# One-operation variances in the tail, half of the h rows ahead of the LN3 sums, and keys of two more pairs on ScalarE

## The chip, the cores and the metric

The kernel runs on one core of a Trainium2 chip. The metric is device time of one execution in microseconds (us); lower is better. The recorded span of an execution is the stretch that the profile covers; the time is about 1.8 us longer. A measurement of the kernel before gave 286.26 us, median of 3 runs, 286.24 to 286.33.

Some words: a look is one profiled execution. The granted clock is the share of its full rate that TensorE was given, by the profile's own record; half clock is 0.50 there and full clock 1.00. A load lands when its completion is signalled, a little after its last packet (0.41 us for the last weights in before, 0.36 us in the look of the tail alone). PSUM is the memory that this kernel's matmuls write into, SBUF the one that its loads land in.

## The reference, cut to what matters

One decode step of one token: attention over a 4096-key window of a cache with 32 heads, then a gated MLP, each behind a layer norm without gain.

```python
x = A_x                                                        # 1 x 1 x 640
h = x + A(layernorm(x), k_cache, v_cache, wq, wo)              # 32 heads of 192, last 4096 keys
h2 = h + B(layernorm(h), w_in, w_sp, b_sp, w_out)
# B: z = gelu(x @ w_in); z1, z2 = halves; z2 = layernorm(z2)
#    g = w_sp * z2 + b_sp  (one token: w_sp and b_sp are scalars);  out = (z1 * g) @ w_out
```

LN1, LN2 and LN3 below are the norms of x, of h and of z2. Most bytes are keys and values: 16 pairs of heads with 3 MB of keys and 3 MB of values each; 119.35 MB are loaded in all.

## The kernel before: what the change and the argument touch

The keys of a pair are multiplied by the query on VectorE, then summed over the 192 channels: by matmuls with the identity on TensorE, with some columns taken over by ScalarE (`BY_ACT`) or VectorE (`BY_DVE`).

```python
BY_ACT = (0, 1, 3, 5, 7, 9, 11)     # 16 of 32 key columns of the first half of these pairs on ScalarE
BY_DVE = (2, 4, 6, 8, 10, 12)

def add_on_act(t, part):            # 8 columns each call, one activation per column
    ...
    for j in range(j0, j0 + JS // 2):
        nc.scalar.activation(out=k3[:, j, :], in_=k3[:, j, :], func=ACT.Copy, accum_out=S[:, j:j + 1])
```

The reciprocal root is an integer seed and two Newton steps, each of two one-column VectorE operations:

```python
def ln_rstd(hv):                    # hv = -variance / 2
    yi = ...                        # seed: tensor_scalar on the bits, two immediate scalars
    for _ in range(2):
        scalar_tensor_tensor(out=t_, in0=y, scalar=y, in1=hv, op0=mult, op1=mult)
        scalar_tensor_tensor(out=yn, in0=t_, scalar=1.5, in1=y, op0=add, op1=mult)
```

The tail after attention (cut):

```python
tensor_scalar(out=h_pc, in0=attn_ps, ..., accum_out=sums2[0])                 # copy of h, and its sum
nc.scalar.activation(out=hsq, in_=attn_ps, func=ACT.Square, accum_out=sums2[1])
matmul(mean_ps, avgD_f, sums2[0]);  matmul(half_ps, halfD_f, sums2[1])        # across the partitions
tensor_scalar(out=hb1, in0=h_pc, scalar1=mean_ps, op0=subtract)
tensor_scalar(out=mh, in0=mean_ps, scalar1=mean_ps, scalar2=0.5, op0=mult, op1=mult)   # LN2
tensor_tensor(out=hv2, in0=mh, in1=half_ps, op=subtract)
rstd2 = ln_rstd(hv2)
z2_ps = half_in(Fh)                                                           # 30 matmuls, z2
activation(out=T3, in_=z2_ps, func=Gelu, scale=rstd2, accum_out=...)
matmul(lin_ps, rootF_f, sums3)                                                # LN3 sums
... # 16 matmuls that add the rows of h to the output
tensor_copy(out=m3, in_=lin_ps)                                               # LN3
scalar_tensor_tensor(out=hv3, in0=m3[:, 0:1], scalar=m3[:, 0:1], in1=m3[:, 1:2], op0=mult, op1=subtract)
activation(out=mw, in_=m3[:, 0:1], ...); activation(out=Tw, in_=T3, scale=.., bias=mw)
rstd3 = ln_rstd(hv3)
tensor_scalar(out=gz, in0=Tw, scalar1=rstd3, scalar2=sp_f[:, 1:2], op0=mult, op1=add)
z1_ps = half_in(0)                                                            # 30 matmuls, z1
activation(out=z1, in_=z1_ps, func=Gelu, scale=rstd2)
tensor_tensor(out=gv, in0=z1, in1=gz, op=mult)
... # 24 matmuls gv x w_out, the copy o_sb, the store
```

## Time and profile before

| what | where it is read | number |
|---|---|---|
| span of the profiled run | top of the page | 285.2 us |
| load queue, share of 16 engines' span | queue table | 97.6% |
| VectorE, TensorE, ScalarE busy | first part of the page | 74%, 60%, 22% |
| 3 MB key tile, issue to landing | issue table | 30.2 us |
| values of the last pair but one (14) in use | chain of waits | 264.69 us |

Lines of the page of before: span, the load queue (packets, MB, share), and the issue group of full key tiles (count, KB each, median us from issue to landing).

```profile
span 285.2 us, 3077 instructions
...
q1 hardware_dynamic: 5384, 119.35, 97.6%
...
k_t<-in_A_k_cache_dram SPq DMA_DIRECT2D x15, 3072.0 KB, 30.2
```

By my estimate, from the 3072 KB of a tile and the 417 to 438 GB/s that the windows of before show between 36 and 240 us, a tile alone would take about 7 us. The 30.2 us from issue to landing are thus mostly a queue of about four tiles, and at 97.6% of their span the load engines are not waiting for anybody.

Lines of the chain of waits of before (start us, length us, what):

```profile
106.06 5.10 PE sc_ps L324 x12
111.22 27.95 DMA k_t<-in_A_k_cache_dram
...
264.69 1.87 PE pv_174 L413 x12
```

The matmul piece ends at 111.16 us in the release of a key buffer, and a load that was issued then, at 111.22, follows. There are such pieces at 106 and at 168 us, and it is tempting to shorten the matmuls of the pairs at these times. But by the same estimate the 28 to 29 us behind them are mostly queueing, so I expected an earlier release mostly to make the queue longer.

Lines of the timeline of before, in the tail (start us, length us, engine, source line, operation, out<-in, sizes, count, in brackets the idle time before and its releaser). L575 is the first copy of h, L585 and L587 are LN2's product and subtraction, L613 and L615 LN3's copy and variance, L225 the seeds, L626 z1's gelu, L623 gz, L628 gv, L634 the output copy:

```profile
275.25 0.17 DVE L575 TENSOR_SCALAR_CACHE_REDUCE h_pc<-attn_ps 128x5 f32<-128x5 f32 x1 [1.09 <-PE attn_ps L479]
...
276.24 0.21 DVE L585 TENSOR_SCALAR mh<-sm_ps 128x1 f32<-128x1 f32 x1
...
276.56 0.16 DVE L587 TENSOR_TENSOR lnv<-mh,sc_ps 128x1 f32<-128x1 f32 x1
276.75 0.15 DVE L225 TENSOR_SCALAR lnyi<-lnv 128x1 int32<-128x1 int32 x1
...
279.14 0.16 DVE L613 COPY lnm<-sm_ps 128x2 f32<-128x2 f32 x1 [0.68 <-PE sm_ps L605]
...
279.34 0.22 DVE L615 SCALAR_TENSOR_TENSOR lnv<-lnm 128x1 f32<-128x1 f32 x1
279.59 0.15 DVE L225 TENSOR_SCALAR lnyi<-lnv 128x1 int32<-128x1 int32 x1
...
280.70 0.27 ACT L626 ACTIVATE z_2034<-sm_ps,lny 128x6 f32<-128x6 f32 x1 [0.64 <-PE sm_ps L594]
280.75 0.29 DVE L623 TENSOR_SCALAR gz<-Tw,lny,sp_f 128x6 f32<-128x6 f32 x1
281.15 0.17 DVE L628 TENSOR_TENSOR gv<-z_2034,gz 128x6 bf16<-128x6 f32 x1
...
282.39 0.32 DVE L634 CAST o_sb<-sc_ps 128x160 bf16<-128x160 f32 x1 [1.08 <-PE sc_ps L631]
```

Here gz is the half z2 after LN3, scaled by w_sp and shifted by b_sp; gv is z1 times gz, the input of the 24 output matmuls. From the first copy of h to gv it is 281.15 - 275.25 = 5.90 us, and from gv to the output copy 1.24 us.

### The profile page before, as it was taken

How to read it: one execution, taken by the hardware profiler on the slowest of the kernel's cores; microseconds unless marked ns; L12 is line 12 of the kernel's file. 1: busy time of each engine (PE TensorE's matmuls, PEld its weight loads, DVE VectorE, ACT ScalarE, POOL GpSimd, SP SyncE). 2: the span in 40 equal slices, each digit the busy share in tenths (PEclk: the TensorE clock that was granted, in tenths of full speed). 3: DMA queues.
4: the chain of work that ended last, by engine and by line, in shares of the span. 5: the costliest groups of instructions: out<-in, count | busy, mean ns of one | idle time of the engine just before them, and what ended most of it. 6: DMA issues, size and time to landing. Idle time of an engine off the chain costs nothing.

```text
span 285.2 us, 3077 instructions
## 1 busy us (share of the span) xinstructions
PE 172.3 (60%) x1134; PEld 67.9 (24%) x1134; DVE 212.3 (74%) x289; ACT 64.1 (22%) x316; POOL 2.3 (1%) x10
## 2 busy tenths in 40 slices
PE   0329935773765369635771587536961785775874
PEld 0103412221222023111230122102321222322463
DVE  7300099899999968998499949996699949995443
ACT  2001347412231431132301440143101010202301
POOL 3000000000000000000000000000000000000000
PEclk9999979799699557975898559955796879989575
DMA  8999999999999999999999999999999999999993
GB/s 331 434 400 434 441 429 401 443 462 434 434 400 443 420 441 434 413 466 407 434 441 434 434 430 441 420 436 441 423 431 425 441 437 411 452 427 416 398 401 123
DMA packets 5405, 119.54 MB, mean 419 GB/s; under 512 B 973, under 2 KB 2254, under 8 KB 2830
## 3 DMA queue, kind: packets, MB, share of 16 engines
q1 hardware_dynamic: 5384, 119.35, 97.6%
q8 instruction: 9, 0.15, 0.2%
q14 instruction: 6, 0.05, 0.0%
q10 hardware_dynamic: 6, 0.00, 0.0%
HBM read 119.34 MB, written 0.00 MB: 418 GB/s over the span
## 4 chain that ended last, share of the span: by engine, by line
DVE 41%; DMA 37%; PE 18%; issue 2%; SPq 1%; ACT 0%; DVEq 0%; ACTq 0%
DVE k_t L317 22%; DMA k_t<-in_A_k_cache_dram 20%; DMA v_t<-in_A_v_cache_dram 11%; PE sc_ps L324 7%; DMA wq_t<-in_A_wq_dram 7%; DVE S L310 5%; PE sc_ps L265 5%; DVE ob L438 4%; DVE S L331 4%; PE pv_174 L413 1%; PE attn_ps L474 1%; PE sm_ps L341 1%; SPq L58 1%; PE pv_176 L403 1%; DVE gm L343 1%
## 5 line engine op out<-in xcount | busy, mean ns | idle before, releaser
L317 DVE TENSOR_TENSOR k_t<-k_t,q_208 128x6144 bf16<-128x6144 bf16 x32 | 107.2, 3352 | 19.5 <-DMA k_t<-in_A_k_cache_dram 19.1
L324 PE MATMUL sc_ps<-k_t,ident_bf 128*128 128x512 bf16 x306 | 93.0, 464 | 47.0 <-DVE k_t L317 47.0
L324 PEld LDWEIGHTS <-ident_bf 128*128 128x128 bf16 x306 | 33.0, 113 | 98.0 <-issue 62.1
L307 ACT ACTIVATE k_t<-k_t 128x192 bf16<-128x192 bf16 x112 | 38.8, 348 | 34.1 <-DVE k_t L317 34.1
L265 PE MATMUL sc_ps<-wq_t,xn_128 128*128 128x512 bf16 x60 | 17.2, 444 | 10.4 <-DMA wq_t<-in_A_wq_dram 7.9
L331 DVE TENSOR_REDUCE S<-sc_ps 128x32 f32<-128x512 f32 (+1 forms) x32 | 21.9, 684 | 1.2 <-PE sc_ps L324 1.2
L307 ACT ACTIVATION_READ_ACCUMULATOR k_t<-k_t 128x1 f32 x112 | 20.9, 186 | 0.0
L310 DVE TENSOR_REDUCE S<-k_t 128x16 f32<-128x3072 bf16 x6 | 20.1, 3349 | 0.0
L273 DVE COPY sp_f<-sm_ps 128x2 f32<-128x2 f32 x1 | 0.2, 159 | 25.0 <-PE sm_ps L271 25.0
L360 ACT ACTIVATE E_125<-S,bias 128x64 bf16<-128x64 f32 x12 | 4.2, 360 | 44.9 <-DVE bias L350 44.9
L360 ACT ACTIVATE E_127<-S,bias 128x64 bf16<-128x64 f32 x10 | 3.5, 360 | 47.9 <-DVE bias L350 47.9
L360 ACT ACTIVATE E_126<-S,bias 128x64 bf16<-128x64 f32 x10 | 3.5, 360 | 45.4 <-DVE bias L350 45.4
L265 PEld LDWEIGHTS <-xn_128 128*128 128x128 bf16 x60 | 6.4, 108 | 20.8 <-issue 13.2
L267 ACT ACTIVATE q_208<-sc_ps 128x512 bf16<-128x512 f32 x6 | 3.6, 597 | 29.9 <-PE sc_ps L265 29.9
L413 PE MATMUL pv_174<-v_t,E_127 128*8 128x512 bf16 (+1 forms) x72 | 7.9, 488 | 3.0 <-DMA v_t<-in_A_v_cache_dram 3.0
L343 DVE TENSOR_REDUCE gm<-sm_ps 2x1 f32<-2x128 f32 x16 | 4.5, 279 | 6.9 <-PE sm_ps L341 6.9
L413 PE MATMUL pv_176<-v_t,E_126 128*8 128x512 bf16 (+1 forms) x72 | 8.1, 492 | 0.7 <-DMA v_t<-in_A_v_cache_dram 0.5
L413 PE MATMUL pv_176<-v_t,E_125 128*8 128x512 bf16 (+1 forms) x48 | 5.8, 521 | 0.9 <-DMA v_t<-in_A_v_cache_dram 0.9
L413 PE MATMUL pv_174<-v_t,E_125 128*8 128x512 bf16 (+1 forms) x72 | 6.2, 424 | 0.0
L413 PE MATMUL pv_176<-v_t,E_127 128*8 128x512 bf16 (+1 forms) x48 | 5.0, 474 | 1.8 <-DMA v_t<-in_A_v_cache_dram 1.8
L413 PEld LDWEIGHTS <-E_127 128*8 128x8 bf16 (+1 forms) x120 | 3.5, 89 | 9.8 <-issue 7.9
L413 PEld LDWEIGHTS <-E_126 128*8 128x8 bf16 (+1 forms) x120 | 3.5, 87 | 6.9 <-issue 4.7
(242 smaller groups left out, 149.6 us busy)
## 6 DMA issues: line engine op xcount, KB each, us to landing
k_t<-in_A_k_cache_dram SPq DMA_DIRECT2D x15, 3072.0 KB, 30.2
v_t<-in_A_v_cache_dram SPq DMA_DIRECT2D x15, 3072.0 KB, 28.6
wq_t<-in_A_wq_dram SPq DMA_DIRECT2D x5, 1536.0 KB, 11.2
wo_t<-in_A_wo_dram SPq DMA_DIRECT2D x7, 960.0 KB, 20.1
k_t<-in_A_k_cache_dram SPq DMA_DIRECT2D x2, 1536.0 KB
v_t<-in_A_v_cache_dram SPq DMA_DIRECT2D x1, 1536.0 KB
w_in_sb<-in_B_w_in_dram SPq DMA_DIRECT2D x2, 576.0 KB, 14.5
wo_t<-in_A_wo_dram SPq DMA_DIRECT2D x2, 480.0 KB, 13.7
```

Of the source, the lines that this page charges most:

```text
L58: eng.add_instruction(mybir.InstDMACopy(name=nc.get_next_instruction_name(), mode="Copy", queue="qSPDynamicHW", ins=eng.lower_ap_dma(in_, ...
L265: nc.tensor.matmul(psv, lhsT=xn2[:, c, a, :], rhs=wc[:, gq:gq + 4, a, w0:w0 + P], start=(c == 0 and a == 0), stop=(c == DC - 1 and a == 1))
L267: nc.scalar.activation(out=q2f[:, gq:gq + 4, w0:w0 + P], in_=psv, func=ACT.Copy, scale=scale)
L307: nc.scalar.activation(out=k3[:, j, :], in_=k3[:, j, :], func=ACT.Copy, accum_out=S[:, j:j + 1])
L310: nc.vector.tensor_reduce(out=st[t]["S"][:, J - JS:J], in_=products(t)[:, J - JS:J, :], axis=AX.X, op=ALU.add)
L317: nc.vector.tensor_tensor(out=kc, in0=kc, in1=q2[:, t:t + 1, :].to_broadcast([P, JC, Dh]), op=ALU.mult)
L324: nc.tensor.matmul(psv, lhsT=ident_bf[:], rhs=products(t)[:, j0:j1, n * g:(n + 1) * g], start=(n == 0), stop=(n == Dh // g - 1))
L331: nc.vector.tensor_reduce(out=S[:, j0:j1], in_=st[t]["ps"][ch], axis=AX.X, op=ALU.add)
L343: nc.vector.tensor_reduce(out=gm[:], in_=mT[0:2, 0:P], axis=AX.X, op=ALU.max)
L360: nc.scalar.activation(out=E[:, :, a], in_=S[:], func=ACT.Exp, bias=bias[:, a:a + 1], accum_out=zq[q][:, a, b:b + 1])
L413: nc.tensor.matmul(pv[p0:p0 + 2 * n, :].rearrange("p (k r i) -> p k r i", k=n, r=32), lhsT=E[:, j0:j0 + n, :].rearrange("p j a -> p (j a)" ...
L438: nc.vector.tensor_reduce(out=ob[:, i0:i0 + ni], in_=flat.rearrange("p (k r i) -> p i r k", k=n, i=ni), axis=AX.X, op=ALU.add)
```

## The change

Its intent: take the variance in one VectorE operation straight from PSUM, with mean and mean square as two per-partition scalars; let TensorE add half of the h rows while it would otherwise wait for LN3's sums; and free TensorE of key sums in pairs 4 and 8, which I took to hold a buffer in the chain. The factor 16 that the new root carries is put into the other scales. Cut to its core:

```diff
+    def neg_var(mean, square):
+        nc.vector.tensor_scalar(out=v[:], in0=mean, scalar1=mean, scalar2=square, op0=ALU.mult, op1=ALU.subtract)
-    BY_ACT = (0, 1, 3, 5, 7, 9, 11)
+    BY_ACT = (0, 1, 3, 4, 5, 7, 8, 9, 11)
     # LN2
-    nc.vector.tensor_scalar(out=mh[:], in0=mean_ps, scalar1=mean_ps, scalar2=0.5, op0=ALU.mult, op1=ALU.mult)
-    nc.vector.tensor_tensor(out=hv2[:], in0=mh[:], in1=half_ps, op=ALU.subtract)
-    rstd2 = ln_rstd(hv2)
+    rstd2 = ln_rstd16(neg_var(mean_ps, square_ps))
     # LN3
+    h_rows(0, NG // 2)
-    nc.tensor.matmul(lin_ps, lhsT=rootF_f[:], rhs=sums3[:], start=True, stop=True)
-    ... all 16 matmuls of the h rows
-    nc.vector.tensor_copy(out=m3[:], in_=lin_ps)
-    nc.vector.scalar_tensor_tensor(out=hv3[:], in0=m3[:, 0:1], scalar=m3[:, 0:1], in1=m3[:, 1:2], ...)
+    nc.tensor.matmul(lin_ps, lhsT=avgF_f[:], rhs=sums3[:], start=True, stop=True)
+    h_rows(NG // 2, NG)
+    v3 = neg_var(lin_ps[:, 0:1], lin_ps[:, 1:2])
```

LN1 gets the same form; one small scale operation is added at the start of the loop.

More of the change, by code (lines that the diff above doesn't have):

```diff
@@ L164 @@
     nc.vector.memset(avgD_f[:], 1.0 / D)
-    halfD_f = const.tile([P, P], F32)
-    nc.vector.memset(halfD_f[:], 0.5 / D)
-    rootF_f = const.tile([P, P], F32)
-    nc.vector.memset(rootF_f[:], 0.5 ** 0.5 / Fh)
+    avgF_f = const.tile([P, P], F32)
+    nc.vector.memset(avgF_f[:], 1.0 / Fh)
     T3 = const.tile([P, FHC + 1], F32)
@@ L221, in ln_sums, with ln_rstd16 @@
         return psv
-    def ln_rstd(hv):
+    def neg_var(mean, square):
+        v = small.tile([P, 1], F32, tag="lnv", name="lnv")
+        nc.vector.tensor_scalar(out=v[:], in0=mean, scalar1=mean, scalar2=square, op0=ALU.mult, op1=ALU.subtract)
+        return v
+    def ln_rstd16(v):
         yi = small.tile([P, 1], I32, tag="lnyi", name="lnyi")
-        nc.vector.tensor_scalar(out=yi[:], in0=hv[:].bitcast(I32), scalar1=-0.5,
-                                scalar2=float(0x5F3759DF - (1 << 30) - (1 << 22)), op0=ALU.mult, op1=ALU.add)
+        nc.vector.tensor_scalar(out=yi[:], in0=v[:].bitcast(I32), scalar1=-0.5, scalar2=float(0x5F3759DF - (1 << 30)),
+                                op0=ALU.mult, op1=ALU.add)
         y = yi[:].bitcast(F32)
-        for _ in range(2):
+        for c_ in (3.0, 12.0):
             t_ = small.tile([P, 1], F32, tag="lnt", name="lnt")
-            nc.vector.scalar_tensor_tensor(out=t_[:], in0=y, scalar=y, in1=hv[:], op0=ALU.mult, op1=ALU.mult)
+            nc.vector.scalar_tensor_tensor(out=t_[:], in0=y, scalar=y, in1=v[:], op0=ALU.mult, op1=ALU.mult)
             yn = small.tile([P, 1], F32, tag="lny", name="lny")
-            nc.vector.scalar_tensor_tensor(out=yn[:], in0=t_[:], scalar=1.5, in1=y, op0=ALU.add, op1=ALU.mult)
+            nc.vector.scalar_tensor_tensor(out=yn[:], in0=t_[:], scalar=c_, in1=y, op0=ALU.add, op1=ALU.mult)
             y = yn[:]
@@ L245 @@
     nc.vector.tensor_reduce(out=mean1[:], in_=ln_sums(x_pc[:], DC, avgD_f), axis=AX.X, op=ALU.add)
-    hv1 = small.tile([P, 2], F32, tag="lnv", name="lnv")
-    nc.vector.tensor_scalar(out=hv1[:], in0=mean1[:], scalar1=0.5, scalar2=None, op0=ALU.mult)
-    nc.vector.scalar_tensor_tensor(out=hv1[:, 0:1], in0=mean1[:, 0:1], scalar=hv1[:, 0:1], in1=hv1[:, 1:2],
-                                   op0=ALU.mult, op1=ALU.subtract)
-    rstd1 = ln_rstd(hv1[:, 0:1])
+    rstd1 = ln_rstd16(neg_var(mean1[:, 0:1], mean1[:, 1:2]))
     for a in range(2):
@@ L266 @@
                                      start=(c == 0 and a == 0), stop=(c == DC - 1 and a == 1))
-            nc.scalar.activation(out=q2f[:, gq:gq + 4, w0:w0 + P], in_=psv, func=ACT.Copy, scale=scale)
+            nc.scalar.activation(out=q2f[:, gq:gq + 4, w0:w0 + P], in_=psv, func=ACT.Copy, scale=scale / 16)
     free("kv", NWQ)
@@ L272 @@
     sp_f = const.tile([P, 3], F32)
-    nc.vector.tensor_copy(out=sp_f[:, 0:2], in_=sp_ps[:, 0:2])
-    nc.vector.tensor_scalar(out=sp_f[:, 2:3], in0=sp_ps[:, 0:1], scalar1=-2.0 ** 0.5, scalar2=None, op0=ALU.mult)
+    for k_, c_, w_ in ((0, 0, 1.0 / 16), (1, 1, 1.0), (2, 0, -1.0 / 16)):
+        nc.vector.tensor_scalar(out=sp_f[:, k_:k_ + 1], in0=sp_ps[:, c_:c_ + 1], scalar1=w_, scalar2=None, op0=ALU.mult)
     attn_ps = psum.tile([P, 512], F32, tag="acc", name="attn_ps", bufs=1)
@@ L579 @@
     nc.tensor.matmul(mean_ps, lhsT=avgD_f[:], rhs=sums2[0][:], start=True, stop=True)
-    half_ps = sc_bank()[:, 0:1]
-    nc.tensor.matmul(half_ps, lhsT=halfD_f[:], rhs=sums2[1][:], start=True, stop=True)
+    square_ps = sc_bank()[:, 0:1]
+    nc.tensor.matmul(square_ps, lhsT=avgD_f[:], rhs=sums2[1][:], start=True, stop=True)
     hb1 = small.tile([P, DC], BF16, tag="hb1", name="hb1", bufs=1)
-    nc.vector.tensor_scalar(out=hb1[:], in0=h_pc[:], scalar1=mean_ps, scalar2=None, op0=ALU.subtract)
-    mh = small.tile([P, 1], F32, tag="mh", name="mh", bufs=1)
-    nc.vector.tensor_scalar(out=mh[:], in0=mean_ps, scalar1=mean_ps, scalar2=0.5, op0=ALU.mult, op1=ALU.mult)
-    hv2 = small.tile([P, 1], F32, tag="lnv", name="lnv")
-    nc.vector.tensor_tensor(out=hv2[:], in0=mh[:], in1=half_ps, op=ALU.subtract)
-    rstd2 = ln_rstd(hv2)
+    nc.vector.tensor_scalar(out=hb1[:], in0=h_pc[:], scalar1=mean_ps, scalar2=1.0 / 16, op0=ALU.subtract, op1=ALU.mult)
+    rstd2 = ln_rstd16(neg_var(mean_ps, square_ps))
     def half_in(f0):
@@ L601, with h_rows @@
     tsq = small.tile([P, FHC + 1], F32, tag="tsq", name="tsq", bufs=1)
-    nc.vector.scalar_tensor_tensor(out=tsq[:], in0=T3[:], scalar=0.5 ** 0.5, in1=T3[:], op0=ALU.mult, op1=ALU.mult,
+    nc.vector.scalar_tensor_tensor(out=tsq[:], in0=T3[:], scalar=1.0, in1=T3[:], op0=ALU.mult, op1=ALU.mult,
                                    accum_out=sums3[:, 1:2])
-    lin_ps = bank()[:, 0:2]
-    nc.tensor.matmul(lin_ps, lhsT=rootF_f[:], rhs=sums3[:], start=True, stop=True)
-    for g in range(NG):
-        for c in range(DC):
-            lo, hi = max(g * OW, c * P), min((g + 1) * OW, (c + 1) * P)
-            if lo < hi:
-                nc.tensor.matmul(orow[32 * g:32 * g + 1, lo - g * OW:hi - g * OW], lhsT=h_pc[:, c:c + 1],
-                                 rhs=ident_f[:, lo - c * P:hi - c * P], start=(lo == g * OW), stop=False)
-    m3 = small.tile([P, 2], F32, tag="lnm", name="lnm")
-    nc.vector.tensor_copy(out=m3[:], in_=lin_ps)
-    hv3 = small.tile([P, 1], F32, tag="lnv", name="lnv")
-    nc.vector.scalar_tensor_tensor(out=hv3[:], in0=m3[:, 0:1], scalar=m3[:, 0:1], in1=m3[:, 1:2],
-                                   op0=ALU.mult, op1=ALU.subtract)
+    def h_rows(g0, g1):
+        for g in range(g0, g1):
+            for c in range(DC):
+                lo, hi = max(g * OW, c * P), min((g + 1) * OW, (c + 1) * P)
+                if lo < hi:
+                    nc.tensor.matmul(orow[32 * g:32 * g + 1, lo - g * OW:hi - g * OW], lhsT=h_pc[:, c:c + 1],
+                                     rhs=ident_f[:, lo - c * P:hi - c * P], start=(lo == g * OW), stop=False)
+    h_rows(0, NG // 2)
+    lin_ps = bank()[:, 0:2]
+    nc.tensor.matmul(lin_ps, lhsT=avgF_f[:], rhs=sums3[:], start=True, stop=True)
+    h_rows(NG // 2, NG)
+    v3 = neg_var(lin_ps[:, 0:1], lin_ps[:, 1:2])
     mw = small.tile([P, 1], F32, tag="mw", name="mw", bufs=1)
-    nc.scalar.activation(out=mw[:], in_=m3[:, 0:1], func=ACT.Copy, scale=sp_f[:, 2:3])
+    nc.scalar.activation(out=mw[:], in_=lin_ps[:, 0:1], func=ACT.Copy, scale=sp_f[:, 2:3])
     Tw = small.tile([P, FHC], F32, tag="Tw", name="Tw", bufs=1)
     nc.scalar.activation(out=Tw[:], in_=T3[:, 0:FHC], func=ACT.Identity, scale=sp_f[:, 0:1], bias=mw[:, 0:1])
-    rstd3 = ln_rstd(hv3)
+    rstd3 = ln_rstd16(v3)
     gz = small.tile([P, FHC], F32, tag="gz", name="gz", bufs=1)
```

## The prediction

The sum stays at about -0.2 us, LN3's 0.19 us (gv from 281.15 to 280.96), and the 286.05 us is that much below the 286.26. That ScalarE's read follows VectorE's is expected from the trace of before, where ScalarE's square of attn_ps starts at 275.45 us, released by VectorE's copy of the same tile, whose second part ends at 275.41. The +/-0.3 us of (a) was an estimate of mine.

> **What bounds the kernel now.** The load stream. The queue table gives the load queue 97.6% of the span; the windows show DMA shares of 0.97 to 1.02 from 22 to 240 us. The issue table gives 28 to 30 us from issue to landing for a 3 MB tile, about four tiles' time: queueing. VectorE is busy 74%, TensorE 60%, ScalarE 22%. In the chain of waits, engine stretches end in buffer releases (106.06-111.22 and 167.79-172.81, key contractions of pairs 4 and 8), each followed by a 28 to 29 us DMA piece. Releasing those buffers earlier only lengthens the backlog. From 264.69, when the values of pair 14 land, a dependent tail of 18 us runs to the output.
>
> **Keys of pairs 4 and 8 on ScalarE.** Removes 6 of 12 contraction matmuls (about 0.43 us each there) in one chunk of each pair. Adds 16 activations per pair at about 0.345 us, 5.5 us, on an engine with room. Both lie behind the saturated queue: 0 us.
>
> **LN1.** One short operation less, done by 9.3 us; the last query weight lands at 21.98: 0 us. The extra scale operation at 35.3, about 0.1 us, is absorbed.
>
> **LN2 (timeline 275-278).** Before: mean product at 276.24 (0.21 us), subtraction at 276.56 (0.16), seed at 276.75. The second sum's matmul runs 275.92 to 276.48, so I read the subtraction as waiting for that matmul, not for the product. The new single operation starts at about 276.53 and takes about 0.22: 0 us, from -0.1 to +0.07.
>
> **LN3 (timeline 278-281).** Before: sums land 279.11, copy 279.14 (0.16), variance 279.34 (0.22), seed 279.59, last Newton step ends 280.65, gz 280.75, gv 281.15. The copy goes: VectorE moves up 0.19. But z1 would then bind: its gelu starts at 280.70 because TensorE did 16 h-row matmuls (279.04-279.77) before the z1 projection, so gv could not start before 281.01. Half of the h rows in TensorE's idle time (277.33-278.52) frees about 0.35 us, z1 is off the path, gv starts at about 280.96. [...]ScalarE's read of the sums should follow VectorE's (trace of before: ScalarE's square waits for VectorE's copy from the same bank). Tw then ends at about 280.1, still ahead of gz.
>
> Sum: about -0.2 us, all in LN3. The down-projection weights land at about 281.0; their last chunk is needed at about 281.8.
>
> **Predicted 286.05 us**, range 285.65 to 286.4. Chances: faster by over 2% 0.01, within 2% 0.98, slower 0.01.
>
> **What would show it.** Chain of waits: values of pair 14 land within 0.3 us of 264.7. Timeline: LN2's seed as long after the mean's matmul as before; LN3 sums to gv shorter by 0.2; z1's gelu no longer adjacent to gv. DMA share unchanged.
>
> **What would make it wrong.** (a) The clock: the windows show 0.50 granted from 266 to 271 and after 275, 0.85 to 1.0 between. [...]a shift could move when the value matmuls at 265-273 speed up, perhaps +/-0.3 us. (b) LN2's subtraction was waiting for the product: up to 0.25 us more gain. (c) The stream's rate changes with the altered engine traffic (0.1% is 0.27 us). (d) Two PSUM scalar operands cost more than 0.22 us.

## The result, and the profile after

The changed kernel took 286.81 us (median of 6 runs, 286.49 to 287.75) against 286.31 us of before in the same rounds (6 runs, 286.24 to 286.72). The ratio was 1.0022 with an interval of 1.0003 to 1.0041. A ratio here is the mean time of one kernel's runs over that of the other's of the same rounds, so not quite the ratio of the medians that are quoted. The prediction of 286.05 us, range 285.65 to 286.4, missed it.

Yet the profiled run of the changed kernel has a shorter span. The span and the load queue, from its page:

```profile
span 284.5 us, 3122 instructions
...
q1 hardware_dynamic: 5384, 119.35, 97.7%
```

Its chain of waits, the pieces that answer to those of before:

```profile
105.20 5.01 PE sc_ps L323 x12
110.28 28.67 DMA k_t<-in_A_k_cache_dram
...
264.24 1.87 PE pv_172 L412 x12
```

The pieces are the same ones. The load queue has the same share of the span. The values of pair 14 are in use at 264.24 us instead of 264.69. The chain still shows the twelve matmuls at 105 us (5.01 us, against 5.10 before), and the others at 167.60 us (4.54 us, against 4.96). They are of pairs 5 and 9, whose keys were summed in the same way before, so the change does not touch them.

The tail after. L574 is the copy of h, L223 the new variance (first LN2's, then LN3's), L228 the seeds, L613 ScalarE's read of the mean, L618 gz, L621 z1's gelu, L623 gv, L629 the output copy:

```profile
274.60 0.17 DVE L574 TENSOR_SCALAR_CACHE_REDUCE h_pc<-attn_ps 128x5 f32<-128x5 f32 x1 [1.18 <-PE attn_ps L478]
...
275.88 0.29 DVE L223 TENSOR_SCALAR lnv<-sm_ps,sc_ps 128x1 f32<-128x1 f32 x1 [0.19 <-PE sc_ps L580]
276.20 0.15 DVE L228 TENSOR_SCALAR lnyi<-lnv 128x1 int32<-128x1 int32 x1
...
278.59 0.29 DVE L223 TENSOR_SCALAR lnv<-sm_ps 128x1 f32<-128x1 f32 x1 [0.68 <-PE sm_ps L609]
278.92 0.15 DVE L228 TENSOR_SCALAR lnyi<-lnv 128x1 int32<-128x1 int32 x1
278.92 0.26 ACT L613 ACTIVATE mw<-sm_ps,sp_f 128x1 f32<-128x1 f32 x1 [1.21 <-DVE lnv L223]
...
280.07 0.29 DVE L618 TENSOR_SCALAR gz<-Tw,lny,sp_f 128x6 f32<-128x6 f32 x1
280.12 0.27 ACT L621 ACTIVATE z_2048<-sm_ps,lny 128x6 f32<-128x6 f32 x1 [0.51 <-PE sm_ps L589]
280.47 0.17 DVE L623 TENSOR_TENSOR gv<-z_2048,gz 128x6 bf16<-128x6 f32 x1
...
281.71 0.33 DVE L629 CAST o_sb<-sc_ps 128x160 bf16<-128x160 f32 x1 [1.08 <-PE sc_ps L626]
```

Measured from the first copy of h, at the same granted clock of 0.50:

| step | before | after | difference |
|---|---|---|---|
| copy of h to LN2's seed | 276.75 - 275.25 = 1.50 | 276.20 - 274.60 = 1.60 | +0.10 |
| variance of LN3 begun (or its copy) to the seed | 279.59 - 279.14 = 0.45 | 278.92 - 278.59 = 0.33 | -0.12 |
| copy of h to gv | 5.90 | 5.87 | -0.03 |
| gv to the output copy | 1.24 | 1.24 | 0 |

So the tail gained 0.03 us where 0.2 us had been predicted. The reason is on the L223 lines: the new operation takes 0.29 us, not 0.22. In LN2 it replaces only the 0.16 us subtraction, since the product had ended in before (276.45 us) when the second sum's matmul did (276.48). The trace of before had hinted at it: L623 (gz), with two per-partition scalars, takes 0.29 us there.

Left to explain: why the one operation is that long, where +0.5 us came from, and whether it exists.

### The profile page after: what moved, and what is told of

Same layout as the page of the kernel before. It is cut to its first block, busy times and chain, and to the rows that moved or that the text cites. A ratio compares the mean times of both kernels' runs of the same rounds, so it can differ in the third digit from the quotient of the medians.

```text
span 284.5 us, 3122 instructions
## 1 busy us (share of the span) xinstructions
PE 174.1 (61%) x1122; PEld 67.9 (24%) x1122; DVE 211.8 (74%) x286; ACT 75.2 (26%) x380; POOL 2.3 (1%) x10
## 3 DMA queue, kind: packets, MB, share of 16 engines
q1 hardware_dynamic: 5384, 119.35, 97.7%
## 4 chain that ended last, share of the span: by engine, by line
DVE 41%; DMA 38%; PE 18%; issue 2%; SPq 1%; ACT 0%; DVEq 0%; ACTq 0%
DVE k_t L316 22%; DMA k_t<-in_A_k_cache_dram 20%; DMA v_t<-in_A_v_cache_dram 11%; DMA wq_t<-in_A_wq_dram 6%; PE sc_ps L323 6%; DVE S L309 5%; PE sc_ps L264 4%; DVE ob L437 4%; DVE S L330 4%; PE attn_ps L473 2%; PE pv_172 L412 1%; PE sm_ps L340 1%; SPq L58 1%; DVE gm L342 1%; PE pv_174 L402 1%
## 5 line engine op out<-in xcount | busy, mean ns | idle before, releaser
L323 PE MATMUL sc_ps<-k_t,ident_bf 128*128 128x512 bf16 x294 | 94.5, 484 | 44.2 <-DVE k_t L316 44.2
L306 ACT ACTIVATE k_t<-k_t 128x192 bf16<-128x192 bf16 x144 | 49.9, 348 | 33.0 <-DVE k_t L316 33.0
L306 ACT ACTIVATION_READ_ACCUMULATOR k_t<-k_t 128x1 f32 x144 | 26.9, 187 | 0.0
L273 DVE TENSOR_SCALAR sp_f<-sm_ps 128x1 f32<-128x1 f32 x3 | 0.3, 152 | 24.6 <-PE sm_ps L270 24.6
```

Source lines behind the costliest of these rows:

```text
L323: nc.tensor.matmul(psv, lhsT=ident_bf[:], rhs=products(t)[:, j0:j1, n * g:(n + 1) * g], start=(n == 0), stop=(n == Dh // g - 1))
```

## The experiments

Theory K: the keys of two more pairs on ScalarE disturb the load stream. Theory S: the constants that moved in memory do. Theory N: nothing of the +0.5 us is due to the change; it is spread from run to run. Theory P: each per-partition scalar operand of a VectorE operation has its price. Theory T: the load stream sets the time, in the tail through the last weights. Theories F and I concern the time beyond the span.

### Before against itself

The kernel before, unchanged.

> The kernel before, unchanged, against itself: what the method calls a difference where there is none, and its spans beside its times. All theories: ratio 1.000. If the ratio's interval or the spread of its runs reaches +/-0.2% (0.5 us), the +0.22% of the change can be chance (theory N, no reproducible loss). Theories K and S below want its runs to stay within 0.1 us of 286.3, as the six runs of before nearly did.

Measured: 286.94 us (6 runs, 286.46 to 288.21) against 286.91 us (11 runs, 286.33 to 287.54); ratio 1.0005, interval 0.9986 to 1.0025. The unchanged kernel spreads over 1.75 us, and the six runs that the change had been compared with were all in the lowest part of that. K's and S's demand that before stay at 286.3 fails.

Run-to-run spread alone is not a likely reason for those six, though: five of them are at 286.39 us or below, and only 2 of the 50 later runs of before are. So something of that first sitting differed. The record names chips 7, 10, 13 and 14 for the later sittings and none for the first. That the change does cost something on the first one's chip is not excluded; no run went back to it.

### The change again

> The changed kernel again. Theory K (the two more pairs on ScalarE cost the load stream something) and theory S (the constants that moved in memory do): ratio again about 1.002, +0.5 us. Theory N (in the tail the change is worth -0.03 us, and the rest of the measured +0.5 us is spread from run to run): ratio within 1.000 +/-0.001, spans about equal to those of the unchanged kernel.

Measured: 286.83 us (5 runs, 286.79 to 286.99); ratio 0.9996, interval 0.9981 to 1.0011. The span is 284.8 us (median), that of before 285.1. As N expected, the first +0.22% did not repeat (on chip 7 here, on 10 and 13 later). What the expectation had wrong: the spans are not equal, and time less span is larger (1.89 to 2.49 us, against 1.74 to 1.91 of before). More on this below.

### The keys alone

```diff
-    BY_ACT = (0, 1, 3, 5, 7, 9, 11)
+    BY_ACT = (0, 1, 3, 4, 5, 7, 8, 9, 11)
```

> Before, with pairs 4 and 8 added to the ScalarE list and nothing else. Theory K: all of the loss is here, +0.5 us (ratio 1.002), and the values of pair 14 land later. Theory S and theory N: 0.0 us (ratio 1.000). In the trace the queue's DMA share stays at about 97.6% by N.

Measured: 287.05 us (6 runs), ratio 1.0011, interval 0.9994 to 1.0029. The load queue's share is 97.7%, and the values of pair 14 are in use at 264.78 us, 0.09 us later than in before. No loss to be told from the spread, and K's +0.5 us (1.002) still lies inside this interval, so this run alone doesn't refute K; the repeats of the whole change (0.9996, 1.0000 and 1.0005) leave nothing that K would have to explain. The 32 activations more (and the 32 reads of their sums) do no visible good either.

### The tail alone

```diff
-    BY_ACT = (0, 1, 3, 4, 5, 7, 8, 9, 11)        # the changed kernel
+    BY_ACT = (0, 1, 3, 5, 7, 9, 11)
```

> After, with the ScalarE list of before: the LN changes, the moved h rows and the moved constants alone. Theory K: -0.03 us. Theory S: +0.5 us. Theory N: -0.03 us, not to be told from 0. In the trace, from the first copy of h to the gv product 5.87 us as in the changed kernel (5.90 before), the two variance operations at 0.29 us each.

Measured: 286.88 us (5 runs), ratio 0.9999, interval 0.9985 to 1.0012. S falls: this kernel has all the moved constants, and the +0.5 us (1.0017) lies outside the interval.

This run and the one before it, of the two halves of the change, happen to have the copy of h at the same time, 275.11 us, and full clock for LN2. They show a second thing. The timeline of the tail alone: copy of h, gv, weight loads of the output matmuls, output copy.

```profile
275.11 0.16 DVE L574 TENSOR_SCALAR_CACHE_REDUCE h_pc<-attn_ps 128x5 f32<-128x5 f32 x1 [1.47 <-PE attn_ps L478]
...
280.65 0.17 DVE L623 TENSOR_TENSOR gv<-z,gz 128x6 bf16<-128x6 f32 x1
280.87 0.62 PEld L626 LDWEIGHTS <-gv 128*1 128x1 bf16 x21 [0.69 <-DVE gv L623]
...
281.71 0.09 PEld L626 LDWEIGHTS <-gv 128*1 128x1 bf16 x3 [0.23 <-issue]
282.06 0.32 DVE L629 CAST o_sb<-sc_ps 128x160 bf16<-128x160 f32 x1 [1.25 <-PE sc_ps L626]
```

The timeline of the keys alone, whose tail is that of before:

```profile
275.11 0.17 DVE L575 TENSOR_SCALAR_CACHE_REDUCE h_pc<-attn_ps 128x5 f32<-128x5 f32 x1 [1.50 <-PE attn_ps L479]
...
280.80 0.17 DVE L628 TENSOR_TENSOR gv<-z,gz 128x6 bf16<-128x6 f32 x1
281.01 0.78 PEld L631 LDWEIGHTS <-gv 128*1 128x1 bf16 x24 [0.79 <-DVE gv L628]
...
282.06 0.32 DVE L634 CAST o_sb<-sc_ps 128x160 bf16<-128x160 f32 x1 [1.10 <-PE sc_ps L631]
```

With full clock for LN2 the new tail brings gv 0.15 us earlier (280.65 against 280.80), and the output copy starts at 282.06 us in both. The 24 output matmuls of the new tail run as 20 and then 4: three of the last four weight loads stand apart, at 281.71 us, after 0.23 us idle. The timeline names no releaser for that wait, but the trace's load records do settle it. The last packet of the output weights ended at 281.31 us, the load landed (its completion was signalled) at 281.67, and the 21st matmul began at 281.71, 0.04 us later. The same 0.04 us stand between landing and 21st matmul in every look whose clock was full at the copy of h, seven in all and with the old, the new and the mixed tail. In all seven the output copy starts 0.39 to 0.40 us after the landing and 6.94 to 6.96 us after the copy of h. So in these looks the landing of the last weights sets the end, whichever tail runs before it, and the 0.15 us were won and given back. With half clock for LN2, as in the two looks of the first comparison, there was room: in before the landing was at 281.62 us and the 21st matmul began at 281.99.

### What a scalar operand costs

Sixty one-column operations while VectorE is idle, six of each of ten forms, for example:

```diff
+nc.vector.tensor_scalar(out=o, in0=src[:, 0:1], scalar1=0.5, scalar2=0.25, op0=ALU.mult, op1=ALU.subtract)   # imm2
+nc.vector.tensor_scalar(out=o, in0=src[:, 0:1], scalar1=s0,  scalar2=0.25, ...)                              # ptr1
+nc.vector.tensor_scalar(out=o, in0=src[:, 0:1], scalar1=s0,  scalar2=s1, ...)                                # ptr2
+nc.vector.tensor_scalar(out=o, in0=ps0, ...)                                          # psum0, psum1, psum2 alike
+nc.vector.tensor_copy(out=o, in_=ps0)                                                 # pcopy
```

> Before, with 60 one-column VectorE operations, six of each of ten forms, in the time before the queries when VectorE is idle. Theory P (each per-partition scalar operand adds about 0.07 us to such an operation, wherever it comes from): no scalar operand 0.15, one 0.22, two 0.29 us, for SBUF and PSUM sources alike. Rival Q (it is PSUM that makes the new operation 0.29 us long): two scalars from SBUF 0.22 or less, PSUM forms longer. The values are thrown away; the output stays right.

The groups of the profile by form (line, engine, operation, out<-in, sizes, count, then busy us in all and mean ns of one, and the idle time before them). L265, L267, L269 have none, one and two per-partition scalars and read SBUF; L271, L273, L275 the same from PSUM:

```profile
L275 DVE TENSOR_SCALAR opsum<-sm_ps 128x1 f32<-128x1 f32 x6 | 1.7, 286 | 0.2
L269 DVE TENSOR_SCALAR optr<-src 128x1 f32<-128x1 f32 x6 | 1.6, 271 | 0.2
...
L273 DVE TENSOR_SCALAR opsum<-sm_ps 128x1 f32<-128x1 f32 x6 | 1.3, 221 | 0.2
...
L267 DVE TENSOR_SCALAR optr<-src 128x1 f32<-128x1 f32 x6 | 1.3, 212 | 0.2
...
L271 DVE TENSOR_SCALAR opsum<-sm_ps 128x1 f32<-128x1 f32 x6 | 0.9, 155 | 0.2
L265 DVE TENSOR_SCALAR oimm<-src 128x1 f32<-128x1 f32 x6 | 0.9, 154 | 0.2
```

From SBUF 154, 212 and 271 ns, from PSUM 155, 221 and 286 ns: 0.06 to 0.07 us for each per-partition scalar, and PSUM adds at most 15 ns. The copy from PSUM took 156 ns. P holds, Q falls. An operation with two such scalars (286 ns) is cheaper than a copy and an operation with one (156 + 221 ns), so LN3 gains. It is dearer than a subtraction with none (153 ns, L281) behind a product that had ended by the second sum, so LN2 loses.

### The h rows back behind the sums

```diff
-    h_rows(0, NG // 2)
     nc.tensor.matmul(lin_ps, lhsT=avgF_f[:], rhs=sums3[:], start=True, stop=True)
-    h_rows(NG // 2, NG)
+    h_rows(0, NG)
```

with the ScalarE list of before.

> Tail of after with all h rows after the sums of LN3 again, and the ScalarE list of before. If moving them mattered (my prediction): z1's gelu starts about 0.35 us later against the sums and gv is bound by it. From the first copy of h to gv: 5.87 us where the gate is gz, up to 5.95 where z1 binds.

Measured (one look): copy of h to gv 280.40 - 274.87 = 5.53 us, against 5.54 in the tail alone at the same full clock; to the output copy 6.95 us in both. Its timeline (L617 gz, L620 z1's gelu, L622 gv):

```profile
280.00 0.29 DVE L617 TENSOR_SCALAR gz<-Tw,lny,sp_f 128x6 f32<-128x6 f32 x1
280.07 0.27 ACT L620 ACTIVATE z<-sm_ps,lny 128x6 f32<-128x6 f32 x1 [0.54 <-PE sm_ps L589]
280.40 0.17 DVE L622 TENSOR_TENSOR gv<-z,gz 128x6 bf16<-128x6 f32 x1
```

z1's gelu ended at 280.34 us, 0.05 us after gz (280.29), and still it is not the gate: gv starts 0.10 us after the end of gz in this look, and so it does in the two looks of the first comparison, with z1 earlier or later. Where z1 really came last (A shorter LN3, below), gv followed it after 0.03 us; here it started 0.06 us after it. So z1 does not bind even with the h rows back. Nor did the move bring z1 forward: from the first h row behind the sums to z1's first matmul it is 0.66 us with all 16 rows there (279.04 to 279.70 in before, 278.42 to 279.08 here) and 0.64 us with 8 (278.48 to 279.12 in the change). The prediction had expected 0.35 us. Why eight rows hold TensorE as long as sixteen was not found. Moving the h rows bought nothing measurable.

### LN2 in two operations again

```diff
-    rstd2 = ln_rstd16(neg_var(mean_ps, square_ps))
+    nc.vector.tensor_scalar(out=mh[:], in0=mean_ps, scalar1=mean_ps, scalar2=None, op0=ALU.mult)
+    nc.vector.tensor_tensor(out=v2[:], in0=mh[:], in1=square_ps, op=ALU.subtract)
+    rstd2 = ln_rstd16(v2)
```

with the ScalarE list of before.

> After's tail with LN2's variance taken again in two operations (the square ahead, off the chain, then a subtraction without scalar operand), and the ScalarE list of before. Theory P: LN2 gets its 0.10 us back, from first h copy to gv about 5.77 us (before 5.90, after 5.87). Theory T (the last weights bind next): the sums move up but the last four of the 24 down-projection matmuls wait, so the end moves by less than the gv does; whole kernel within 0.1% of before.

Measured: copy of h to gv 280.70 - 275.00 = 5.70 us, to the output copy 6.95 us; 286.73 us (6 runs), ratio 0.9998, interval 0.9982 to 1.0014. The granted clock fell to half only at 275.3 us here, so some of the 0.17 us against the change is the clock's. The last four matmuls waited a little in this look too: the last weights landed at 281.55 us, the 21st matmul began at 281.59, and the output copy (281.95) is 0.40 us behind the landing as in the other looks of this kind. So T's part of the expectation is met. The version is not to be told from before in time.

### Fifteen pairs on ScalarE

```diff
-    BY_ACT = (0, 1, 3, 5, 7, 9, 11)
+    BY_ACT = tuple(range(15))
```

> Before, with pairs 0 to 14 all on the ScalarE list (eight more pairs, 256 more activations). Theory T (the load stream sets the time): span unchanged to 0.2 us, ratio 1.000. Theory F (the time beyond the recorded span, 1.8 us in 17 runs of before and 2.1 to 2.3 in the changed kernel, grows with ScalarE's program): time less span above 2.3 us, ratio 1.002 or more at the same span.

Measured: 289.03 us (6 runs), ratio 1.0069, interval 1.0048 to 1.0090; the span is 2.2 us longer (287.25 us, median), time less span 1.76 to 1.82 us. Both expectations are hit only in half: T's unchanged span is wrong, F's longer time beyond the span too. F falls, for this kernel has far more activations than the changed one. Where the 2 us come from had to be asked next. In the look of this kernel the values of pair 14 are in use 0.9 us later than in before, and the stretch from there to the copy of h takes 11.77 us at a granted clock of 0.56 (10.56 us at 0.66 in before), so the clock has a part in it that no run separates.

### Twelve pairs on ScalarE

```diff
-    BY_ACT = (0, 1, 3, 5, 7, 9, 11)
+    BY_ACT = tuple(range(12))
```

> Before, with pairs 0 to 11 all on the ScalarE list: five more pairs, where the slower kernel with 0 to 14 had eight more. Theory T (in the loop the load stream sets the time, ScalarE's keys are only in the way at the end): ratio within 1.000 +/-0.001, the last pairs' keys (12 to 14) having cost the 2.0 us. Rival (every further pair on ScalarE costs some 0.25 us): +1.2 us, ratio 1.004.

Measured: 287.04 us (6 runs, 286.74 to 288.35), ratio 1.0007, interval 0.9984 to 1.0031. Five more pairs within the loop cost nothing clear of the spread, a whole 1.2 us is excluded. So it is the last pairs, 12 to 14, that cost. That this is because the queue no longer covers the engines near the end is my reading, which no run shows. Which operation there costs how much, and how much of it is the clock, was not separated.

### More bytes

The input projection's 1.97 MB are loaded twice, once more in the middle of the loop.

```diff
+        if t_ == 8:
+            for a, b in ((0, 3), (3, DC)):
+                plan.append(("w", lambda a=a, b=b: load(w_in_sb[:, a:b, :], win_v[:, a:b, :])))
```

> Before, with the 1.97 MB of the input projection loaded twice, once more among the value and key tiles of pair 8. No other work changes. Theory T (the stream sets the time): +4.5 us (1.97 MB at the 432 GB/s of the loop), ratio 1.016. Rival (the engines' chain through the loop sets it): 0 to 0.5 us.

Measured: 292.05 us (4 runs), ratio 1.0183, interval 1.0157 to 1.0209: +5.3 us. Its timeline, the first matmul on the values of pair 14:

```profile
269.30 1.04 PE L416 MATMUL pv<-v_t,E 128*8 128x512 bf16 x12 [1.71 <-DMA v_t<-in_A_v_cache_dram]
```

It waited for the load of those values and starts 4.61 us later than in before (264.69 us). The last packet of weights ends at 285.84 us instead of 281.21, 4.63 us later. That is the 4.5 us that T expected. The other 0.7 us are the tail behind it (0.6 us longer up to the copy of h in this look) and a longer time beyond the span (2.14 to 2.29 us). 1.6% more bytes make 1.8% more time, while five more pairs on ScalarE made no difference clear of the spread: T holds.

### A shorter LN3

The mixed kernel with one Newton step in LN3 instead of two (two VectorE operations fewer; scales adjusted).

```diff
-    rstd3 = ln_rstd16(v3)
+    rstd3 = ln_rstd16(v3, (3.0,))
```

> Mixed, with one Newton step less in LN3 (scale adjusted; still close, the result may be a little less exact). The chain from sums to gv gets 0.42 us shorter, so first h copy to gv about 5.35 us, unless z1's gelu takes over as gate at about 5.6. Theory T (the last weights bind next): the final output copy follows gv by 1.4 us or more instead of 1.24, the last four matmuls waiting for the last chunk, and the end moves by 0.1 to 0.2 us. Rival (the chain alone sets the end): copy 1.24 us after gv, time -0.3 to -0.5 us against before.

Measured: 286.69 us (6 runs), ratio 0.9995, interval 0.9970 to 1.0021. Its timeline (L574 copy of h, L622 gz, L625 z1's gelu, L627 gv, L633 output copy):

```profile
275.79 0.17 DVE L574 TENSOR_SCALAR_CACHE_REDUCE h_pc<-attn_ps 128x5 f32<-128x5 f32 x1 [1.08 <-PE attn_ps L478]
...
280.74 0.29 DVE L622 TENSOR_SCALAR gz<-Tw,lny,sp_f 128x6 f32<-128x6 f32 x1
281.22 0.27 ACT L625 ACTIVATE z<-sm_ps,lny 128x6 f32<-128x6 f32 x1 [0.52 <-PE sm_ps L593]
281.52 0.17 DVE L627 TENSOR_TENSOR gv<-z,gz 128x6 bf16<-128x6 f32 x1 [0.49 <-ACT z L625]
...
282.76 0.33 DVE L633 CAST o_sb<-sc_ps 128x160 bf16<-128x160 f32 x1 [1.08 <-PE sc_ps L630]
```

gz is done at 281.03 us, but gv waits for z1's gelu until 281.49: the second gate, which the expectation had named as possible. Copy of h to gv is 5.73 us, at half clock, against 5.87 in the change. The output copy follows gv by 1.24 us, so the wait for the weights did not show here: this tail was late for another reason (below), and the last packet of the weights had ended at 281.21 us. As a test of T in the tail this run missed its mark. As a kernel it is again not to be told from before.

### What makes the spread

No run was made for this; it is read from the traces. From the first matmul on the values of pair 14 to the copy of h:

| look | granted clock in that stretch | us |
|---|---|---|
| change, third time | 0.83 | 10.33 |
| tail alone; keys alone | 0.74; 0.75 | 10.33; 10.33 |
| change | 0.66 | 10.36 |
| before | 0.66 | 10.56 |
| short LN3; more bytes | 0.69; 0.69 | 11.11; 11.14 |
| twelve pairs; fifteen pairs | 0.57; 0.56 | 11.74; 11.77 |
| mixed | 0.83 | 10.12 |
| before against itself | 0.66 | 10.35 |

The windows of the change, third time, and of the twelve pairs, over just this stretch (start:end, length, busy us of each engine with instructions, granted clock, load share, GB/s):

```profile
264.68:275.01 10.33, 8.59 (x168) 5.27 (x167) 3.89 (x9) 2.63 (x6) 0.00 (x0) 0.83 0.99 404
```

```profile
264.85:276.59 11.74, 10.19 (x168) 6.64 (x167) 5.03 (x12) 2.91 (x6) 0.00 (x0) 0.57 1.00 400
```

The clock records of before and of the change show two states, 1.00 and 0.50. But for the last piece, which the end of the record cuts, their pieces last 3.41 us or multiples of it (up to 20.48 us), and begin at another point in each: the half-clock piece over the first of these matmuls begins at 264.47 us in before and at 263.43 in the change. How the clock tells on short matmuls is seen in LN2: from the first of its mean to the VectorE operation that waits for them it is 0.63 us at 0.50 (before, 275.47 to 276.10) and 0.42 us at 1.00 (the tail alone, 275.34 to 275.76). In the twelve-pairs look the clock fell to half at 266.4 us and stayed there, in the third look of the change it rose to full at 268.1. Differences of 0.8 to 1.4 us in this stretch are several times anything that the change does. That the clock is their cause is argued from these looks, not shown: no run here set the clock, and how often it lies badly is not known. The stretch is not in proportion to the mean clock: 0.69 goes with a longer one than 0.66, and before has 10.56 and 10.35 us at the same 0.66. Several looks stop at 10.33 us, which would fit a floor set by the landing of the last values, but the mixed kernel's has 10.12.

### The time beyond the span

Over four comparisons the changed kernel has spans of 284.8 us (median of 23 runs); before has 285.0 (the 50 later runs). Time less span is 2.05 us (1.83 to 3.15) and 1.82 us (1.74 to 1.91). The 0.2 us that the span is shorter do not reach the time. One suspicion was that TensorE's program, 24 instructions shorter, moved the last fetch of a piece of program behind the end: the page of the change lists 8 fetches of a program queue in the span, that of before 9.

```diff
+    for i in range(12):
+        nc.tensor.matmul(xc_ps[:, 8 + i:9 + i], lhsT=ones_bf[0:1, :], rhs=ones_bf[0:1, 0:1], start=True, stop=True)
```

In the changed kernel:

> The changed kernel with 12 one-column matmuls into an unused part of a bank, done by 4 us while TensorE is idle: TensorE's program is as long as before again. Theory I (the 12 matmuls fewer moved the last fetch of a piece of the program to after the last result, and that is the 0.25 us beyond the span): time less span back at 1.8 us in all runs, the program queue's 16 KB fetches in the span 9 again. Rival (it comes with ScalarE's longer program, or with nothing): 2.0 us and more, as in 16 of 17 runs of the changed kernel.

In the kernel with the keys alone:

> Before with the two more pairs on ScalarE and the same 12 small matmuls. Without them time less span ran from 1.67 to 2.18 us. Theory I: 1.75 to 1.9 in all runs. Rival: the same scatter. Span as before's to 0.2 us, by theory T.

The changed kernel beside them, unpadded:

> The changed kernel beside it on the same chip. Time less span 2.0 to 2.3 us (median 2.06 in 17 runs so far); ratio to before 1.000 +/-0.002, span 0.2 us below before's. Theory I: after_pad is about 0.2 us faster than this run in the same rounds.

Measured, time less span: padded change 1.84 to 2.11 us (median 2.06), change 1.83 to 2.20 (median 2.04), keys alone padded 1.64 to 1.79. The padded change does have its 9 fetches again, and the extra time stays. Theory I falls for the changed kernel. The other pages say the same: the unpadded change has 9 fetches in its third look, and 8 fetches went with 1.83 us in its fourth and with 1.75 and 1.80 us in the looks of the twelve and the fifteen pairs. (The expectation's "16 of 17" is a slip: by the record 13 of these 17 runs have 2.0 us or more.) Of the halves of the change, the tail alone has 1.84 to 1.90 us and the keys alone 1.67 to 2.18. The times are 287.11, 287.06 and 286.63 us, the ratios 1.0004, 1.0005 and 0.9989, and each interval includes 1. What the 0.2 us beyond the span are stays open.

### The change, third time

> The changed kernel for the third time, on what may be another chip. Theory N (no difference that repeats): interval of the ratio includes 1.000, median within 0.3 us of before's of the same rounds. If the first +0.22% was real (rival): ratio 1.002 again with the interval clear of 1. Time beyond the span: 2.0 to 2.3 us as twice before, if that belongs to this kernel; 1.8 if not.

Measured: 286.88 us (6 runs), ratio 1.0000, interval 0.9979 to 1.0020, time less span 1.83 to 2.71 us.

## Why the prediction was wrong, point by point

In short, three steps failed. The new variance was put at 0.22 us and takes 0.29, so LN2 lost 0.10 us and LN3 gained 0.12 instead of 0.19. The last weights, taken to land early enough, set the end in every look with full clock at the copy of h. And the base of 286.3 us did not hold: in the later sittings the kernel before has 286.8.

- *The load stream bounds the kernel, and the keys of pairs 4 and 8 are worth 0 us.* Right. The queue's share stays at 97.7%; 1.97 MB more cost 5.3 us; twelve pairs on ScalarE change nothing clear of the spread.
- *The pieces of the chain at 106 and 168 us are pairs 4 and 8, which the change would shorten.* Wrong, without consequence for the sum. The matmuls of these pieces follow the projection that runs once every two pairs, behind the odd ones, so they are the second halves of pairs 5 and 9, with twelve matmuls before and after (5.10 and 5.01 us, 4.96 and 4.54 us).
- *LN1 and the scale operation are worth 0 us.* Not contradicted: the stream's share and the pieces of the chain are unchanged. They were not run alone.
- *LN2: 0 us, from -0.1 to +0.07, with the new operation at about 0.22 us.* That the subtraction waited for the second sum at half clock is not settled by the trace: in before the product ended at 276.45 us, the second sum's matmul at 276.48, the subtraction started at 276.56, and the chain of waits goes through the product. The new operation did start hardly earlier after the copy of h than the subtraction had (275.88 - 274.60 = 1.28 us, against 1.31). The size was off: the operation takes 0.29 us and LN2 lost 0.10 us. With full clock for LN2 the tail alone has its seed 1.27 us after the copy of h, the keys alone 1.30 us: there the product is on the chain (in the keys alone the second sum's matmul ended at 276.01 us, the product at 276.12, and the subtraction followed at 276.22), which was point (b) of the prediction, but its gain was 0.03 us and not up to 0.25.
- *LN3: VectorE moves up 0.19 us.* Mis-sized by the same term: (d) of the prediction came true. The step from sums to seed gained 0.12 us.
- *Without the h rows moved z1 would bind; moving them frees it.* Wrong in both halves. Without the move gv still follows gz by the usual 0.10 us (5.53 us after the copy of h, against 5.54 with it), and the move brought z1's first matmul forward by 0.02 us, not 0.35.
- *ScalarE's read of the mean follows VectorE's.* Right: L613 starts at 278.92 us, released by L223, which ends at 278.88, and Tw ended at 279.60, 0.47 us before gz began.
- *The last weights don't take the gain back.* Wrong in the looks with full clock for LN2. The tail's gain there was 0.15 us, and the four last matmuls waited that much: they start 0.04 us after the landing. I had compared two numbers of a single execution, 281.0 and 281.8, of which both move.
- *About -0.2 us in sum.* Measured up to gv: -0.03 us at half clock, -0.15 us with full clock for LN2, and 0 at the output copy there.
- *286.05 us, 285.65 to 286.4.* This was the larger fault. It was set on three runs within 0.09 us of each other, although the profiled execution of the same kernel, beside them, took 287.0 us. All 56 runs of before have a median of 286.78 us and go from 286.24 to 288.21. A kernel equal to before belongs at 286.8, and the changed one has 286.90 us (median of 23 runs). The range should have held the clock's spread, which point (a) named at +/-0.3 us and for which the looks give 0.8 to 1.4 us, if the clock is its cause. Why the first six runs of before were so low stays open.

As to the first comparison (1.0022, interval clear of 1): three repeats gave 0.9996, 1.0000 and 1.0005. The change is neither a gain nor a loss that the later runs can show; the first sitting, with its low runs of before, was not repeated. No version tried here beats both kernels; the lowest ratio is 0.9989, of the keys alone with twelve idle matmuls, and its interval (0.9972 to 1.0005) includes 1.

## What to carry to other kernels

Count operands, not only operations: here merging two short vector operations gained where both ran after the last input (LN3, 0.12 us) and lost where one had ended before it (LN2 at half clock, 0.10 us), since each per-partition scalar that the merged one added cost 0.06 to 0.07 us. This kernel streams its loads to the end and its tail raced the last bytes: in the tail alone the last weights landed at 281.67 us, 0.04 us before the 21st of the 24 matmuls that use them. In such a kernel, ask how long after the last landing the chain really ends before shortening it. And run the unchanged kernel against itself, in more than one sitting, before believing a few tenths of a percent.
